# Stage two's way-back products in two halves of 64 stationary columns

## The chip, the cores and the metric

The kernel runs on one core of a Trainium2 chip. The metric is the device time of one execution in microseconds (us); what is compared is the median of several runs. The core's engines run side by side, each with its own order of instructions: PE (TensorE: matmuls, and beside them PEld, the load of the stationary operand), DVE (VectorE), ACT (ScalarE), POOL (GpSimd), and SP, which issues DMA transfers, as ACT and POOL do too. Operands lie in SBUF, an on-chip memory of 128 partitions; matmuls write to PSUM, whose banks hold 512 float32 values in each of 128 partitions.

A matmul `matmul(out, a, b)` computes the transpose of `a` times `b`. `a` is the stationary operand: its columns are loaded into the array and become the partitions of `out`. `b` is the moving operand: its columns stream through. In the profile `128*64 128x512` is a matmul with 128 partitions and 64 stationary columns, through which 512 moving columns stream.

## The reference

A block with two parts on `x` of 2048 rows and 512 columns: a spectral filter between two normalisations, then a dense layer with Mish and another dense layer. The change touches the first part alone.

```python
def _A_ref(x, w_r, w_i):
    X = rfft2(x, axes=(-2, -1))
    X = X * (w_r + 1j * w_i)
    return irfft2(X, s=(S, D), axes=(-2, -1))
...
h = _layernorm(x, axis=-1) * (1 + ca) + sa
x = x + ga * _A_ref(h, A_w_r, A_w_i)
h = _layernorm(x, axis=-1) * (1 + cb) + sb
x = x + gb * _B_ref(h, B_w1, B_b1, B_w2)
```

All inputs and outputs are float32.

## The kernel before

The two-dimensional Fourier transform is split into matmuls with small tables. Stage one (to about 50 us) takes the rows apart and does a transform of length 128 over the partitions; its result for each of 64 frequencies q of the row transform lies in the tile `a_sb`, 128 values in each of 128 partitions.

Stage two (about 50 to 90 us) works on groups of these frequencies, listed in `groups`: group 0 holds q = 0, group 1 the three of q = 1 to 3, and fifteen further groups hold four each. `seq` is the order in which they are taken: 1, 2, 3, 4, 0, 5, and so on. For each group, in this order:

- `p2_in` (L521) transposes the group's frequencies by four matmuls with `ident` (L528) into a bank "A", and ACT copies them out (L531). POOL adds a small correction to one column (L539).
- `p2_mul` (L541) multiplies by the table `kf`: one matmul with 512 moving columns (L548) into a bank "B" or "C".
- `p2_prod` (L562) multiplies by the spectral weights, a complex product: ACT copies the halves with their parts exchanged (L579, L580), POOL and DVE multiply (L581, L582).
- `p2_add` (L585): DVE adds the two products into the group's own place in `a_sb` (L588).
- `p2_out` (L590): the way back. For each of the group's `nq` frequencies a matmul (L597) with the 128 columns of that frequency in `a_sb` as the stationary operand and the first 128 columns of the table `kv` as the moving one. They write the columns `i * P` to `(i + 1) * P` of one bank "D", of which there are two. P is 128.
- `store_d` (L432) empties that bank into the tiles `dd[0]` and `dd[1]`, with a negated copy of a part: ACT by L441 and L443, in some groups DVE by L439 and L445 and POOL by L447.

Group 0 has its own way through `z_in`, `z_mul`, `z_prod`, `z_back` and `z_out`. `z_mul` and `z_out` call `reflected` (L463), which adds up several products in one bank: L464 and L468 with 128 stationary columns, L465 with a single column that writes one partition, and in `z_out` L467, whose operands have 96 partitions.

The order of the work is written out by hand: the loop over `s` at L648 is a software pipeline, and each engine works through its instructions in the order in which this loop issues them. In step `s` PE gets the table product of group `seq[s + 1]`, then the transposes of group `seq[s + 4]`, then the way-back products of group `seq[s - 3]`. From s = 13 on no transposes are left, and from s = 16 on no table products: the way-back products of the last five groups (s = 15 to 19) follow one another. DMA transfers of spectral weights (L630) are issued from ACT's queue within the same loop, as are those of the table `kc` (L686).

Stage three (from about 90 us) first does the column products of the inverse transform (L830 and L831, which read `dd` and `kc`), the row products (L840), and then both dense layers, whose matmuls (L942, L1045 and others) fill the time up to the end. Its order is a list of steps, `ORDER`, sorted by hand; the change doesn't touch it.

The change stands in `p2_out`. In the profile a product of float32 operands is two records, each with a weight load; so the 63 products of L597 are 126 matmuls and 126 weight loads.

Of the kernel before, what the change touches and what calls it, by code (L numbers as in the profile page):

```python
# [12 lines left out]
P = 128  # L13
# [69 lines left out]
def tile_spectral_block(ctx: ExitStack, tc: tile.TileContext, x_d, w1_d, b1_d, w2_d,  # L83
                        c_d, xt_d, wm_d, wq_d, wz_d, kr_d, km_d, kc_d, ki_d, kf_d, kv_d, kw_d, kp_d, out_d):
    nc = tc.nc
# [26 lines left out]
    def bank(tag):  # L112
        return psum.tile([P, 512], F32, name="bank", tag=tag)
# [38 lines left out]
    kv = pw.tile([P, 512], F32, name="kv")  # L152
# [279 lines left out]
    def store_d(ps, q0, nq, kind="all"):  # L432
        src = ps[:, 0:nq * 128].rearrange("p (q a c) -> p a c q", q=nq, c=2)
        for i in range(2):
            dst = dd[i].rearrange("p n d c q -> p (n d) c q")
            s = src[:, 32 * i:32 * i + 32]
            to, minus = dst[:, :, 0:2, q0:q0 + nq], dst[:, :, 2, q0:q0 + nq]
            if kind == "free" and i:
                nc.vector.tensor_copy(to, s)  # L439
            else:  # L440
                nc.scalar.copy(to, s)  # L441
            if kind == "all":
                nc.scalar.mul(minus, s[:, :, 0, :], -1.0)  # L443
            elif kind != "pool" and i:
                nc.vector.tensor_scalar(minus, s[:, :, 0, :], -1.0, None, op0=ALU.mult)  # L445
            else:
                nc.gpsimd.tensor_scalar(minus, dst[:, :, 0, q0:q0 + nq], -1.0, None, op0=ALU.mult)  # L447
# [67 lines left out]
    def z_out():  # L515
        t1, t2 = st.pop(("t", 0))
        pe = bank("D")
        reflected(pe[:, 0:P], t1, lambda i: kv[:, 128 + i * P:256 + i * P], [(t2[0:96, 0:P], kw)])
        store_d(pe, 0, 1)
# [33 lines left out]
    def slot(g):  # L553
        q0, nq = groups[g]
        return a_sb[:, q0:q0 + nq].rearrange("p q n e -> p (q n e)")
# [34 lines left out]
    def p2_out(g, kind):  # L590
        if g == 0:
            return z_out()
        q0, nq = groups[g]
        y = slot(g)
        pd = bank("D")
        for i in range(nq):
            nc.tensor.matmul(pd[:, i * P:(i + 1) * P], y[:, i * P:(i + 1) * P], kv[:, 0:128],  # L597
                             start=True, stop=True)
        store_d(pd, q0, nq, "all" if nq < 4 else kind)

    late = {}
# [30 lines left out]
    with tc.manual_schedule():  # L632
# [15 lines left out]
        for s in range(1, len(seq) + 3):  # L648
# [26 lines left out]
            if s >= 3:  # L675
                p2_out(seq[s - 3], "all" if s > 15 else "pool" if s > 13 else "busy" if work_mod[s] else "free")
# [566 lines left out]
    start = {}  # L1243
# [239 lines left out]
```

## Time and profile before

| | |
|---|---|
| time, median of three runs | 372.47 us (372.26 to 372.69) |
| the profiled execution | 372.4 us |
| its span, first to last instruction | 370.5 us |
| mean granted TensorE clock | 0.997 of full speed |
| PE busy | 363.6 us, 98% of the span |
| DVE, ACT, POOL busy | 309.9, 253.6, 64.8 us |
| way-back products, L597 | 126 matmuls of 272 to 377 ns, between 58.6 and 89.7 us |

Rows of the profile read as follows. A row of a timeline gives the start in us from the first instruction, the length in us, the engine, the line of the kernel, the operation, its output and inputs by name, their shapes, and how many instructions are merged in the row; in brackets stands how long the engine was idle before it and what ended that idle time. A row of grouped instructions gives after the bar the busy time in us and the mean length of one in ns, and then the idle time before them. A row of a stretch gives its bounds in us, its length, and for each engine the busy time and the number of instructions, and at the end the granted clock, the busy share of the DMA engines and the rate in GB/s. "issue" as a releaser is time in which the engine waited for nothing that the profile shows. Matmuls are pipelined and their ends are modelled, so the difference between starts says more than the length.

### The profile page before, as it was taken

What the parts mean: (1) busy time and instruction counts of PE and PEld (TensorE: products, weight loads), DVE (VectorE), ACT (ScalarE), POOL (GpSimd) and SP (SyncE); (2) the same over time, 40 slices, a digit from 0 to 9 for tenths busy, and PEclk for the clock granted to TensorE, in tenths of its full rate; (3) what the DMA queues carried; (4) which work ended last, traced back from release to release, by engine and by line L of the source; (5) the groups of instructions that cost most, each with busy time, mean ns of one, the idle gap of its engine ahead of it and who ended that gap; (6) DMA issues with size and microseconds to landing.
All of it is one profiled execution on the core that took longest, in us unless ns stands there. A gap on an engine that the chain in (4) does not pass through costs nothing.

```text
span 370.5 us, 8169 instructions
## 1 busy us (share of the span) xinstructions
PE 363.6 (98%) x2884; PEld 348.6 (94%) x2884; DVE 309.9 (84%) x760; ACT 253.6 (68%) x553; POOL 64.8 (17%) x102
## 2 busy tenths in 40 slices
PE   8999999998999999999999999999999999999995
PEld 8989977777999999999999999999999999999994
DVE  1898967888898899999898868996768978867896
ACT  1698879996557789789575778765686744555750
POOL 0478738786000000000001000000000000000000
PEclk9999999999999999999999999999999999999998
DMA  7999998777624656856978699775996797936032
GB/s 233 380 340 350 346 389 264 239 177 288 230 85 143 227 193 226 284 178 222 316 237 219 199 282 271 238 211 168 291 303 224 196 306 227 296 121 176 15 58 113
DMA packets 50888, 85.79 MB, mean 232 GB/s; under 512 B 7169, under 2 KB 18529, under 8 KB 50593
## 3 DMA queue, kind: packets, MB, share of 16 engines
q1 hardware_dynamic: 47680, 74.65, 60.2%
q10 hardware_dynamic: 2160, 6.95, 6.0%
q0 software_dynamic: 1008, 3.67, 5.9%
q8 instruction: 23, 0.38, 0.4%
q14 instruction: 17, 0.13, 0.1%
HBM read 66.12 MB, written 15.47 MB: 220 GB/s over the span
## 4 chain that ended last, share of the span: by engine, by line
PE 84%; DVE 7%; ACT 5%; issue 2%; ACTq 1%; POOL 0%; DVEq 0%
PE bank L942 28%; PE bank L1045 24%; PE bank L830 4%; PE bank L840 4%; PE bank L831 4%; PE bank L258 4%; PE bank L991 3%; PE bank L303 3%; PE bank L1041 3%; ACT buf L580 1%; PE bank L314 1%; PE bank L305 1%; PE bank L304 1%; ACT buf L579 1%; ACT d L441 1%
## 5 line engine op out<-in xcount | busy, mean ns | idle before, releaser
L1097 POOL DMA_DIRECT2D x<-modr x7 | 6.2, 888 | 260.2 <-DVE st L172 104.5
L942 PE MATMUL bank<-hT,wr 128*128 128x256 f32 x360 | 51.7, 283 | 0.0
L942 PEld LDWEIGHTS bank<-hT,wr 128*128 128x128 f32 x360 | 46.9, 192 | 0.1
L942 PE MATMUL bank<-hB,wr 128*128 128x256 f32 x300 | 43.4, 284 | 0.0
L942 PEld LDWEIGHTS bank<-hB,wr 128*128 128x128 f32 x300 | 39.1, 191 | 0.0
L1045 PE MATMUL bank<-w2a,ah 128*128 128x256 f32 x161 | 35.3, 283 | 0.0
L878 DVE TENSOR_TENSOR al<-buf,ah 128x512 fp32r<-128x512 f32 (+1 forms) x45 | 29.7, 666 | 4.6 <-ACT ah L877 4.5
L1045 PE MATMUL bank<-w2b,ah 128*128 128x256 f32 x147 | 32.3, 283 | 0.0
L877 ACT CAST ah<-buf 128x512 fp32r<-128x512 f32 (+1 forms) x45 | 26.9, 602 | 5.6 <-PE bank L1045 3.2
L942 PE MATMUL bank<-hcr,wr 128*128 128x256 f32 x210 | 30.0, 283 | 0.0
L942 PEld LDWEIGHTS bank<-hcr,wr 128*128 128x128 f32 x210 | 27.2, 192 | 0.0
L1045 PEld LDWEIGHTS bank<-w2a,ah 128*128 128x128 f32 x161 | 26.8, 192 | 0.0
L830 PE MATMUL bank<-kc,d 128*128 128x128 f32 x128 | 24.9, 276 | 0.5 <-ACT d L441 0.5
L831 PE MATMUL bank<-kc,d 128*128 128x128 f32 x128 | 24.7, 275 | 0.0
L1045 PEld LDWEIGHTS bank<-w2b,ah 128*128 128x128 f32 x147 | 24.6, 191 | 0.0
L1045 PE MATMUL bank<-w,ah 128*128 128x256 f32 x112 | 22.0, 286 | 0.0
L172 DVE BATCH_NORM_STATS2 st<-x 128x6 f32<-128x512 f32 x32 | 21.9, 685 | 0.0
L303 PE MATMUL bank<-buf,mring 128*128 128x512 f32 x48 | 20.6, 430 | 0.2 <-DVE buf L296 0.2
L830 PEld LDWEIGHTS bank<-kc,d 128*128 128x128 f32 x128 | 19.4, 192 | 0.7 <-ACT d L441 0.7
L831 PEld LDWEIGHTS bank<-kc,d 128*128 128x128 f32 x128 | 19.4, 192 | 0.0
L597 PEld LDWEIGHTS bank<-kv,a_sb 128*128 128x128 f32 x126 | 15.4, 191 | 2.7 <-issue 2.2
L833 ACT COPY buf<-bank 128x512 f32<-128x512 f32 x16 | 9.3, 583 | 12.5 <-PE bank L831 12.5
(295 smaller groups left out, 1099.1 us busy)
## 6 DMA issues: line engine op xcount, KB each, us to landing
wr<-w_S SPq DMA_DIRECT2D x60, 256.0 KB, 3.7
wr<-w_A SPq DMA_DIRECT2D x45, 256.0 KB, 4.1
w_S<-hT SPq DMA_DIRECT2D x20, 256.0 KB, 2.0
x<-in_A_x_dram SPq DMA_DIRECT2D x16, 256.0 KB, 5.1
xring<-in_x_t_dram SPq DMA_DIRECT2D x16, 256.0 KB, 5.0
w_A<-wr SPq DMA_DIRECT2D x15, 256.0 KB, 2.6
x<-modr POOLq DMA_DIRECT2D x7, 512.0 KB, 5.6
out_dram<-x SPq DMA_DIRECT2D x7, 512.0 KB, 3.8
```

The lines of the kernel that those rows point to most:

```text
L172: nc.vector.bn_stats(t, x[:, n, :])
L258: nc.tensor.matmul(pgv[:, j], data(j), krs[:, j, :].rearrange("p (c q) -> p c q", c=2), start=True, stop=True)
L303: nc.tensor.matmul(pa, m[:, a, 0:128], g, start=(i == 0), stop=False)
L597: nc.tensor.matmul(pd[:, i * P:(i + 1) * P], y[:, i * P:(i + 1) * P], kv[:, 0:128], start=True, stop=True)
L830: nc.tensor.matmul(o, dj[:, 0:128], kc[0][:, n, :], start=True, stop=False)
L831: nc.tensor.matmul(o, dj[:, 64:192], kc[1][:, n, :], start=False, stop=True)
L840: nc.tensor.matmul(px[:, j * P:(j + 1) * P], e[:, j * P:(j + 1) * P], kiv[:, j, :], start=True, stop=True)
L877: nc.scalar.copy(h, r)
L878: nc.vector.tensor_tensor(l, r, plain(h), op=ALU.subtract)
L942: nc.tensor.matmul(o, w[:, p, k, :], h[:, q, k, :], start=(first and n == 0), stop=(last and n == 5), skip_group_check=True)
L991: nc.tensor.matmul(o, w1s[:, p, k, :], slots[f"B{k // 2 + 1}{s + 1}"][:, q, k % 2, :], start=(u == 0 and m == 0), stop=(m == 11), skip_gro ...
L1045: nc.tensor.matmul(out_ps[b][n][:, 256 * half:256 * half + 256], a[p][:, e], w2[t][q][:, r], start=(t == 1 and half == 0 and i == 0), stop ...
```

## The change

Each way-back product is issued as two: the first with the stationary columns 0 to 63 of the frequency, which writes partitions 0 to 63 of the output, the second with columns 64 to 127, which writes partitions 64 to 127. The moving operand is the same 128 columns of `kv` for both, and the columns of the bank are the same. The products are the same numbers as before. There are 126 products in place of 63; nothing else is different.

```diff
         for i in range(nq):
-            nc.tensor.matmul(pd[:, i * P:(i + 1) * P], y[:, i * P:(i + 1) * P], kv[:, 0:128],
-                             start=True, stop=True)
+            for lo in (0, P // 2):
+                nc.tensor.matmul(pd[lo:lo + P // 2, i * P:(i + 1) * P], y[:, i * P + lo:i * P + lo + P // 2], kv[:, 0:128],
+                                 start=True, stop=True)
         store_d(pd, q0, nq, "all" if nq < 4 else kind)
```

## The prediction

> **What bounds the kernel now.** I first read the page's head for the engine that is full, then the busy time by stretch for where it is full, then the matmul timeline for how it is filled.
>
> ```profile
> span 370.5 us, 8169 instructions
> PE 363.6 (98%) x2884; PEld 348.6 (94%) x2884; DVE 309.9 (84%) x760; ACT 253.6 (68%) x553; POOL 64.8 (17%) x102
> ```
>
> ```profile
> core 0: us, PE busy (x) PEld busy (x) DVE busy (x) ACT busy (x) POOL busy (x), PEclk, DMA share, GB/s
> 58.40:83.83 25.43, 25.43 (x159) 18.83 (x158) 21.66 (x51) 24.39 (x57) 20.66 (x36) 1.00 0.74 225
> 72.00:74.19 2.19, 2.19 (x17) 1.66 (x15) 1.59 (x3) 2.13 (x5) 1.74 (x4) 1.00 0.91 286
> 83.83:90.40 6.57, 5.24 (x42) 4.69 (x41) 6.36 (x12) 4.78 (x19) 4.33 (x7) 1.00 0.86 339
> 90.40:366.00 275.60, 275.60 (x2304) 274.38 (x2305) 236.85 (x583) 182.62 (x388) 6.99 (x8) 1.00 0.68 209
> ```
>
> PE is busy for 98% of the span. In the part of stage two that holds the first eleven groups of way-back products (58.40 to 83.83) it has no gap, and in everything after stage two (90.40 to 366.00) it has none either. Only the end of stage two, 83.83 to 90.40, leaves PE 1.33 us idle. The granted clock is 1.00 in all four, so no stretch here runs at a lower one. A busy PE may still be waiting inside its pipeline, so the starts decide:
>
> ```profile
> start us, us, engine line op out<-in xcount [idle before <-releaser]
> ...
> 57.47 0.44 PE L464 MATMUL bank<-kf,early 128*128 128x160 f32 x2
> 57.84 0.43 PE L465 MATMUL bank<-kf,early 128*1 128x160 f32 x2
> 58.20 0.54 PE L468 MATMUL bank<-kf,early 128*128 128x160 f32 x2
> 58.58 0.83 PE L597 MATMUL bank<-kv,a_sb 128*128 128x128 f32 x6
> 59.25 1.02 PE L548 MATMUL bank<-early,kf 128*128 128x512 f32 x2
> ...
> 62.74 0.27 PE L506 MATMUL bank<-ident,buf 128*128 128x128 f32 x1
> 62.84 0.27 PE L507 MATMUL bank<-ident,buf 128*96 128x128 f32 x1
> 62.95 1.06 PE L597 MATMUL bank<-kv,a_sb 128*128 128x128 f32 x8
> ...
> 67.34 0.39 PE L464 MATMUL bank<-kv,early 128*128 128x128 f32 x2
> 67.65 0.38 PE L465 MATMUL bank<-kv,early 128*1 128x128 f32 x2
> 67.96 0.49 PE L467 MATMUL bank<-kw,early 96*128 96x128 f32 x2
> 68.29 0.39 PE L468 MATMUL bank<-kv,early 128*128 128x128 f32 x2
> 68.51 1.02 PE L548 MATMUL bank<-buf,kf 128*128 128x512 f32 x2
> ...
> 74.19 1.06 PE L597 MATMUL bank<-kv,a_sb 128*128 128x128 f32 x8
> 75.08 1.02 PE L548 MATMUL bank<-buf,kf 128*128 128x512 f32 x2
> 75.94 0.60 PE L528 MATMUL bank<-ident,a_sb 128*128 128x128 f32 x4
> 76.38 1.06 PE L597 MATMUL bank<-kv,a_sb 128*128 128x128 f32 x8
> ...
> 82.08 1.05 PE L597 MATMUL bank<-kv,a_sb 128*128 128x128 f32 x8
> 82.97 1.02 PE L548 MATMUL bank<-buf,kf 128*128 128x512 f32 x2
> 83.83 4.26 PE L597 MATMUL bank<-kv,a_sb 128*128 128x128 f32 x32
> 88.81 1.13 PE L597 MATMUL bank<-kv,a_sb 128*128 128x128 f32 x8 [0.72 <-DVE a_sb L588]
> 90.40 0.49 PE L830 MATMUL bank<-kc,d 128*128 128x128 f32 x2 [0.46 <-ACT d L441]
> ```
>
> Starts matter here, not lengths: a matmul's length (1.06 for eight) holds its way through the array, which the next one overlaps. A float32 product stands in the trace as two records. One steady step goes from 74.19 to 76.38: eight L597 records to 75.08 (0.89 us), two L548 records to 75.94 (0.86), four transposes to 76.38 (0.44). The sum is the step, 2.19 us, so PE sets it. ACT is busy for 2.13 of such a step, only 0.06 behind. That is why the page's chain of waits passes much of this stage through ACT. A step made shorter would gain 0.06 at most, while a PE made slower is followed at once.
>
> **What a record costs.** Eight L597 records in 0.89 us are 0.111 us each, whole products 0.222. The change makes four records out of two: the same 128 moving columns twice, with 64 stationary columns each time.
>
> ```profile
> L597 PEld LDWEIGHTS bank<-kv,a_sb 128*128 128x128 f32 x126 | 15.4, 191 | 2.7 <-issue 2.2 <-ACT d L443 0.3 <-DVE d L445 0.2
> L991 PEld LDWEIGHTS bank<-hB,w1s 128*96 128x96 f32 x48 | 6.0, 163 | 0.0
> L465 PEld LDWEIGHTS bank<-kv,early 128*1 128x1 f32 x2 | 0.1, 80 | 0.1
> L465 PE MATMUL bank<-kv,early 128*1 128x128 f32 x2 | 0.4, 270 | 0.0
> ```
>
> A weight load becomes cheaper: 80 ns for 1 column, 163 for 96, 191 for 128 give 0.87 ns a column, so some 135 ns for 64, an estimate from these rows. A matmul record doesn't: with one stationary column L465 still lasts 270 ns against L597's 275 or so, and its pair lasts 0.38, so the second starts 0.11 after the first. The streaming of 128 moving columns sets the pace, and a narrower stationary side saves none of it.
>
> No row shows two half-width records on opposite halves, so the price of a split product has two ends. If the second half runs entirely beside the first, it is 0.222 as before, two records of 0.111 in each half, side by side. If one follows the other, it is 4 x 0.111 = 0.444. Less than 0.222 I exclude, since each half still streams two records of 0.111. I take 0.444: the nearest row is L465's, a narrow record that takes its full turn, and no row of this trace shows two matmuls abreast.
>
> **What entering and leaving costs.** L465 is also the one place where the used part of the array shrinks to a few columns and grows again. In the group from 67.34 to 68.51 four products of two records would need 8 x 0.111 = 0.89; they take 1.17, so 0.28 more. In the group from 57.47 to 58.58 three products with 160 moving columns would need 6 x 0.139 = 0.83; they take 1.11, again 0.28 more. At the entry the first record starts at 67.65, not at 67.56 (0.09 late); the other 0.19 is at the way out, where the wide weights aren't loaded ahead. With 96 columns no such delay shows: L507 starts 0.10 after L506, and L597 0.11 after L507. I put the same price on each group of split products. Its first weights add the difference of 64 columns over one (135 - 80 = 0.055 us), since they are loaded behind the drained array: 0.335 us in all, of which 0.145 at the entry. Its lower bound is nothing, if the stall belongs to L465's sharing its output addresses with L464; the upper bound is this price at every change of half (a rival below).
>
> **The sum.** The first eleven groups (one of three products from 58.58, ten of four, the last from 82.08) each have another kind of PE work before and behind them.
> - Ten groups of four: 8 more records, 0.89, and 0.335: 1.225 each, 12.25.
> - The group of three: 0.67 (58.58 to 59.25) becomes 1.33; with 0.335, 1.0.
> - The end: five groups follow one another from 83.83, with one entry for all. Before, 83.83 to L830's start at 90.40 took 6.57, with PE waiting for DVE before the last group. After: 0.145 + 5 x 1.78 + 0.70 (from the last record's turn, 88.81 + 0.89 = 89.70, to 90.40) = 9.75, so +3.18. The exit's 0.19 lies inside the 0.70, in which PE waits for ACT.
>
> ```profile
> 87.97 0.69 DVE L588 TENSOR_TENSOR a_sb<-bank,buf 128x512 f32<-128x512 f32 x1
> ```
>
> ```profile
> 88.56 0.38 ACT L441 COPY d<-bank 128x256 f32<-128x256 f32 x1
> 88.81 0.31 ACT L443 ACTIVATE d<-bank 128x128 f32<-128x128 f32 x1
> ```
>
> DVE's last sum is ready at 88.66, 4.83 after the last L548 has had its turn; the slower PE asks for it after 0.145 + 4 x 1.78 = 7.27. That wait is gone, and PE sets the end as well. ACT empties half a group's bank in some 0.56 us (88.56 to the end of L443 at 89.12), both halves in 1.1, less than the 1.78 that PE takes for a group, so bank D's two buffers hold nothing up.
>
> Together 12.25 + 1.0 + 3.18 = 16.4 us. What else the change moves costs nothing: no DMA, no copy, no wait is added, and the copies of store_d, the weight fetches on ACT's queue and POOL's sums have 1.2 us more per step than now. Since PE has no gap from 90.40 to 366.00, what stage two loses cannot be made up, and the shift reaches the end whole. The profiled execution took 372.4 us, 1.9 around its span of 370.5, and the median of the runs is 372.47. So the forecast is 388.9 us (372.47 + 16.4).
>
> **The rivals.**
> - *The halves run abreast.* Split product 0.222, plus one record (0.111) at a group's end that has no partner, plus 0.335: 0.445 for each of eleven groups, 4.9; at the end only the last record, 0.1, since the wait for DVE stays. +5.0, 377.5. For it: the two halves share no output partition and no stationary column. Against: no row shows it. The Trainium skill has this as a rule (TensorEngine Tiling (Array Packing), Key Properties): different tiles of the array load weights and multiply in parallel. By that rule the time would be this rival's; no run here shows it so far.
> - *Half abreast.* The second half's weights (0.055) are loaded only once the record before has begun, and likewise back: 0.055 + 0.111 per half, 0.332 a product. Groups of four 0.44 + 0.335, of three 0.33 + 0.335: 8.4; the end 0.145 + 5 x 1.33 + 0.70 - 6.57 = 0.9. +9.3, 381.8.
> - *Each change of half drains the array* (0.145, as at L465's entry). Seven changes in a group of four, five in one of three, 39 at the end: +10.15, +0.73 and +5.66 on top of 16.4: 33 us, 405. Against: L465 is a change of width, and the halves are equal. The skill speaks against it too: the same section has the drain at a change of the tiling mode, not of the tile. The 0.28 us at L465 agree with its first half; nothing here shows the second.
> - *The split doesn't reach the array*: half records run as full-width ones, without entry or exit, as the 96-column loads do. 9.57 + (5 x 1.78 + 0.70 - 6.57) = 12.6, 385.1.
> - *Not slower.* The halves run abreast and the drain belongs to L465's shared addresses alone; the unpartnered record is then overlapped by the next L548. Each group costs nothing, 372.5. It decides as long as entry, exit and the last record stay below 0.067 us a group (0.2% of the time, 0.74 us, over eleven); ACT's 2.13 in a step of 2.19 caps a gain near 0.06 a step, some 0.5 us. Against: the same 0.28 in both groups with L465, while L467 and L468 share addresses too and L468 starts without delay.
>
> **Chances.** The forecast 0.43, abreast 0.28, half abreast 0.13, drain at each change 0.05, no split in the array 0.04, not slower 0.07. The range reaches from below the abreast case (377.5) to above the forecast: 376.5 to 391. It leaves out the drain case and the last one, 0.12. About 0.2% is what a measurement of this kernel tells from no change: faster 0.02 and same 0.05 from the last case, slower 0.93.
>
> **What would show it.** L597 should have 252 records of each kind, weight loads near 135 ns, matmuls still near 275. The step from one L597 group to the next should be 3.4 us (2.19 now); 2.6 speaks for abreast, 3.0 for half abreast, 4.4 for a drain at each change. Within a group, the starts should be 0.111 apart with no overlap between halves; pairs that start together would refute me. A gap of about 0.15 before the group's first record and 0.19 behind its last would bear out the entry and exit. L830 should start near 106.8, without the 0.72 wait for DVE, and the stretch behind it should last as long as now. A group that takes 0.9 to 1.0 us would make the prediction wrong at its largest term.

## The result and the profile after

The changed kernel took 375.03 us in the median of four runs (374.69 to 375.55), the kernel before 372.51 (372.26 to 372.69): a ratio of 1.0069 with a 95% interval of 1.0053 to 1.0085. It is slower by 2.5 us. The prediction had the sign, but 16.4 us and a range from 376.5 that leaves 375.03 out.

The head of the page of the changed kernel, and its two groups of way-back products (L598 is the old L597; lines behind it are one higher too), with the matmuls of the kernel before as the last row:

```profile
span 372.9 us, 8421 instructions
PE 366.6 (98%) x3010; PEld 346.8 (93%) x3010; DVE 310.2 (83%) x760; ACT 253.8 (68%) x553; POOL 65.0 (17%) x102
```

```profile
L598 PE MATMUL bank<-kv,a_sb 128*64 128x128 f32 x252 | 16.8, 279 | 0.1
L598 PEld LDWEIGHTS bank<-kv,a_sb 128*64 128x64 f32 x252 | 13.4, 136 | 4.4 <-ACT d L441 1.5 <-issue 1.0 <-DVE bank L582 0.8
...
L597 PE MATMUL bank<-kv,a_sb 128*128 128x128 f32 x126 | 16.6, 277 | 0.9 <-DVE a_sb L588 0.7
```

There are twice as many records, each weight load lasts 136 ns (estimated: 135), each matmul about as long as before (279 ns, 277). Yet together they keep PE busy for 16.8 us, against 16.6 before. The matmul timeline of the changed kernel, a steady step and the end of stage two (start, length, engine, line):

```profile
73.58 1.13 PE L548 MATMUL bank<-buf,kf 128*128 128x512 f32 x2
74.54 0.60 PE L528 MATMUL bank<-ident,a_sb 128*128 128x128 f32 x4
75.07 1.09 PE L598 MATMUL bank<-kv,a_sb 128*64 128x128 f32 x16
76.10 1.12 PE L548 MATMUL bank<-buf,kf 128*128 128x512 f32 x2
...
81.13 1.13 PE L548 MATMUL bank<-buf,kf 128*128 128x512 f32 x2
...
83.21 1.13 PE L548 MATMUL bank<-buf,kf 128*128 128x512 f32 x2
84.27 1.09 PE L598 MATMUL bank<-kv,a_sb 128*64 128x128 f32 x16
85.29 1.13 PE L548 MATMUL bank<-buf,kf 128*128 128x512 f32 x2
86.35 5.13 PE L598 MATMUL bank<-kv,a_sb 128*64 128x128 f32 x80
91.95 0.49 PE L831 MATMUL bank<-kc,d 128*128 128x128 f32 x2 [0.47 <-ACT d L441]
```

Sixteen records take 1.09 us from the first start to the last end, where eight took 1.06. The step, from 73.58 to 76.10, is 2.52 us (2.19 before). The first records of one group, in a stretch cut just behind the first start and in a longer one:

```profile
75.07 0.32 PE L598 MATMUL bank<-kv,a_sb 128*64 128x128 f32 x1
...
75.07 0.33 PE L598 MATMUL bank<-kv,a_sb 128*64 128x128 f32 x2
```

One record reaches to 75.39, two to 75.40: both start within 0.01 us. The rows don't name the half of a record, but two records of one half never start that close (they are 0.109 us apart, see run 1 below), so these two belong to different halves. The halves run abreast, from the first record on; eight pairs follow one another at 0.109 us.

What is left of the 2.52 us is the change of width. The fourth transpose's turn ends at 74.54 + 0.44 = 74.98, and the first pair starts 0.09 later. From it to the next L548 are 1.03, where eight pairs need 0.87: 0.05 for the first narrow load, which nothing covers, and 0.10 before the wide product starts. That product then lasts 1.12 to 1.13 in place of 1.02, as its own first load is uncovered. Together 0.09 + 0.16 + 0.11 = 0.36, less 0.02 for the slightly quicker pairs: the 0.33 us by which the step grew.

Stage two in both profiles, cut at the first L464, the start of the last L548 record, and the first column product of stage three (the first two rows are of the kernel before, the others of the changed one; columns as in the prediction's stretches):

```profile
57.47:83.40 25.93, 25.93 (x164) 19.20 (x162) 22.19 (x51) 24.85 (x59) 20.80 (x37) 1.00 0.75 227
83.40:90.40 7.00, 5.67 (x43) 4.80 (x41) 6.66 (x14) 5.21 (x19) 4.76 (x8) 1.00 0.85 337
```

```profile
56.30:85.83 29.53, 29.53 (x250) 18.83 (x248) 23.45 (x53) 25.67 (x60) 21.83 (x39) 1.00 0.69 212
85.83:91.95 6.12, 5.52 (x83) 4.29 (x81) 5.17 (x11) 4.42 (x18) 3.49 (x6) 1.00 0.83 317
```

The head grew by 3.6 us, eleven times 0.33; the end shrank by 0.9, where PE's idle time fell from 1.33 to 0.60. The sum, 2.7, is the 2.5 us of the runs. The two spans differ by 2.4, since besides stage two began 1.17 us earlier and stage three lasted 0.85 longer (280.95 against 280.11); experiment 4 and the other profiles show both to vary.

What PE waits for at the end is no longer DVE. DVE's last sum is ready 4.21 us after the start of the last L548 record, where it was 5.26, and so in time for the last group. The wait that is left among the way-back products is for a bank D that ACT has still to empty; the kernel before had one like it (0.34 us):

```profile
89.41 1.82 PEld L598 LDWEIGHTS bank<-kv,a_sb 128*64 128x64 f32 x32 [0.37 <-ACT d L443]
```

So the prediction's "bank D's two buffers hold nothing up" held only for the slow groups that it expected.

### The profile page after: what moved, and what is told of

Read it like the earlier page. It is cut to its first block, busy times and chain, and to the rows that moved or that the text cites. A ratio compares the mean times of both kernels' runs of the same rounds, so it can differ in the third digit from the quotient of the medians.

```text
span 372.9 us, 8421 instructions
## 1 busy us (share of the span) xinstructions
PE 366.6 (98%) x3010; PEld 346.8 (93%) x3010; DVE 310.2 (83%) x760; ACT 253.8 (68%) x553; POOL 65.0 (17%) x102
## 4 chain that ended last, share of the span: by engine, by line
PE 88%; DVE 7%; DMA 2%; issue 1%; ACT 1%; DVEq 0%; ACTq 0%
PE bank L943 26%; PE bank L1046 22%; PE bank L548 4%; PE bank L831 4%; PE bank L841 4%; PE bank L832 4%; PE bank L598 4%; PE bank L258 4%; PE bank L992 3%; PE bank L303 3%; PE bank L1042 2%; PE bank L528 2%; DMA w_S<-hT 2%; PE bank L305 1%; PE bank L304 1%
## 5 line engine op out<-in xcount | busy, mean ns | idle before, releaser
L879 DVE TENSOR_TENSOR al<-buf,ah 128x512 fp32r<-128x512 f32 (+1 forms) x45 | 29.7, 665 | 4.6 <-ACT ah L878 4.5
L598 PEld LDWEIGHTS bank<-kv,a_sb 128*64 128x64 f32 x252 | 13.4, 136 | 4.4 <-ACT d L441 1.5
```

The lines of the kernel that those rows point to most:

```text
L598: nc.tensor.matmul(pd[lo:lo + P // 2, i * P:(i + 1) * P], y[:, i * P + lo:i * P + lo + P // 2], kv[:, 0:128], start=True, stop=True)
L879: nc.vector.tensor_tensor(l, r, plain(h), op=ALU.subtract)
```

## The experiments

All of them in one table, from their profiles; "head", "end" and "stage three" are cut as above, "step" is from one L548 to the next in the steady part. Ratios are to the kernel before on the same chip, with their intervals; without one, the time is of a single run. Each run's stages are read from one profile.

| run | step | head | end | stage two | stage three | time, ratio |
|---|---|---|---|---|---|---|
| before | 2.19 | 25.93 | 7.00 | 32.9 | 280.1 | 372.51 |
| the change | 2.52 | 29.53 | 6.12 | 35.7 | 281.0 | 375.03, 1.0069 (1.0053 to 1.0085) |
| 1 low halves first | 3.01 | 34.7 | 7.6 | 42.2 | 280.8 | 381.93, 1.0252 (1.0216 to 1.0288) |
| 2 one product of a group | 2.53 | 29.7 | 7.0 | 36.7 | 280.7 | 376.53, 1.0094 (1.0066 to 1.0121) |
| 3 wide column | 2.19 | 25.8 | 7.4 | 33.2 | 281.3 | 373.19, 1.0008 (0.9994 to 1.0023) |
| 4 before again | 2.19 | 25.9 | 7.1 | 33.0 | 281.2 | 373.45 |
| 5 first eleven groups | 2.52 | 29.5 | 6.1 | 35.6 | 281.4 | 377.21, 1.0098 (1.0066 to 1.0130) |
| 6 last five groups | 2.19 | 25.9 | 7.0 | 32.9 | 280.6 | 372.33, 0.9983 (0.9962 to 1.0004) |
| 7 every other product | 2.87 | 33.4 | 8.9 | 42.4 | 281.1 | 382.67 |
| 8 two by two | 2.57 | 30.0 | 6.2 | 36.3 | 280.9 | 376.02 |
| 9 narrow table product | 2.47 | 28.5 | 7.1 | 35.6 | 280.7 | 375.35 |
| 10 quarters | 2.50 | 29.4 | 6.4 | 35.7 | 281.2 | 375.27 |
| 11 wide column, copies moved | 2.19 | 25.8 | 7.5 | 33.4 | 280.6 | 373.56, 1.0023 (1.0008 to 1.0037) |
| 12 one copy moved | 2.19 | 25.9 | 7.0 | 32.9 | 281.2 | 372.97, 0.9996 (0.9983 to 1.0009) |

**1. How the halves come abreast.**

```diff
-        for i in range(nq):
-            for lo in (0, P // 2):
+        for lo in (0, P // 2):
+            for i in range(nq):
```

> The same products as the change, but all low halves of a group first, then all its high halves. Theory 1 (TensorE picks records for the two halves only among near neighbours in the order): eight records of one half follow one another at 0.109 us, then eight of the other, so a group takes about 1.75 us and the step 2.52 + 0.87 = 3.4 us; eleven steps and the end make about +13 us on 375.0, near 388. Theory 2 (a record of 64 columns lasts half as long whatever its neighbours): the records follow at 0.055, the step stays at 2.52 and the time near 375. Theory 3 (each half has a queue of its own that looks past eight records of the other): pairs as now, step 2.52, near 375, but with low and high records starting together.

None of the three. The step came to 3.01 us. The steady group of this run, whole, and in two stretches from its start, of 0.43 and 0.50 us:

```profile
72.67 1.58 PE L598 MATMUL bank<-kv,a_sb 128*64 128x128 f32 x16
74.19 1.13 PE L548 MATMUL bank<-buf,kf 128*128 128x512 f32 x2
...
72.67 0.65 PE L598 MATMUL bank<-kv,a_sb 128*64 128x128 f32 x4
...
72.67 0.82 PE L598 MATMUL bank<-kv,a_sb 128*64 128x128 f32 x6
```

Four records start alone, the second 0.16 us behind the first and the others 0.109 apart. Then the fifth low record and the first high one, which is ninth in the order, start within 0.01 us of each other (the fifth and sixth record of the last row). From there on low and high run abreast, and the last four high ones are alone: twelve turns in place of eight, 4 x 0.109 = 0.44 of the 0.49 by which the step grew over 2.52. The other 0.05 fits a first load of the high half that nothing covers: the second high record, too, starts 0.16 behind the first. So records of one half do follow one another at the full 0.109, and a high record may start ahead of low ones that stand before it in the order, but here no more than four records ahead: the ninth beside the fifth.

**8. The reach tested.** Low, low, high, high for two frequencies at a time:

```diff
-        for i in range(nq):
-            for lo in (0, P // 2):
+        for i, lo in [(i, lo) for k in range(0, nq, 2) for lo in (0, P // 2) for i in range(k, min(k + 2, nq))]:
+            if True:
```

> All products are split, in the order low, low, high, high for two frequencies at a time, so that four records of one half stand together (two with the change, eight with all low halves first). With all low first, the first high record started beside the fifth low one, as if PE looked past four records. If that is the reach, four records together are still within it: the first high record starts beside the first low one, or one record later at most, and the step stays at 2.52 to 2.63 us. If the reach depends on the halves of a whole group, the first high record starts beside the third low one, and the step is 2.74.

The step was 2.57 and the first high record, fifth in the order, started 0.014 us behind the first low one. Like the ninth beside the fifth in run 1, the fifth beside the first agrees with a reach of four records. Run 10 below shows that it isn't a plain distance in the order.

**2 and 7. Is it the narrow records or the change of width?** Only the last product of a group split, and every other one (both against the kernel before):

```diff
-            nc.tensor.matmul(pd[:, i * P:(i + 1) * P], y[:, i * P:(i + 1) * P], kv[:, 0:128],
-                             start=True, stop=True)
+            wide = P if i < nq - 1 else P // 2
+            for lo in range(0, P, wide):
+                nc.tensor.matmul(pd[lo:lo + wide, i * P:(i + 1) * P], y[:, i * P + lo:i * P + lo + wide], kv[:, 0:128],
+                                 start=True, stop=True)
```

> Only the last product of each group is split, the others keep 128 stationary columns. Theory A (the cost is the entry to and the exit from the narrow form, once per group): the group still pays 0.33 us, the step stays near 2.52 us and the time near 375. At the end, where five groups follow one another, each has its own entry and exit now (five instead of one), so up to 1 us more there. Theory B (each narrow record costs a little): a quarter of the cost, a step of 2.27 us and a time near 373.1.

> In each group every other product is split (0 and 2), the products 1 and 3 keep 128 stationary columns: half as many narrow records as in the change, but two entries and two exits per group. Theory A: twice 0.33 us per group, a step of 2.19 + 0.66 = 2.85 us (2.52 with the change), and about 3.6 us more than the change, near 378.5. Theory B: half of the change's cost, a step of 2.35.

(Experiment 7 has `i % 2` for the condition.) A quarter of the narrow records cost as much per step as all of them, 2.53 us; half of them, in two stretches, cost twice as much over 2.19: 2.87. That is theory A to 0.02 us. At the end run 2 paid its 0.9 for five entries in place of one. Run 7 missed its total, 382.67 against 378.5: I had counted the eleven groups of the head alone, and at the end two entries and exits in each of five groups took another 2.8 us over the change's 6.12. Of the 4.2 us missed, another 0.3 lies in the head, and 1.1 outside stage two, where single executions vary.

**3. Is the delay at L465 the same thing?** L465 multiplies by 128 columns, of which 127 are zero, and not by one. This is against the kernel before; the lines by which POOL prepares `column` are left out:

```diff
-        nc.tensor.matmul(out[0:1], t[:, 0:1], w(2), start=False, stop=False)
+        nc.tensor.matmul(out, column, w(2), start=False, stop=False)
```

> The kernel before, with L465's single stationary column replaced by 128 columns of which 127 are zeros; three small POOL operations and one more memset prepare them. The output addresses are still shared with L464 and L468. Theory A (the delay at L465 comes from the change of width): both groups lose their 0.28 us, 0.83 and 0.89 remain, and the time falls by 0.5 us or less, to about 372.0. Theory C (the delay comes from adding onto the addresses that L464 has just written): nothing changes, 1.11 and 1.17 us remain and the time stays at 372.5.

The later of the two groups in this run:

```profile
67.02 0.39 PE L464 MATMUL bank<-kv,early 128*128 128x128 f32 x2
67.24 0.39 PE L465 MATMUL bank<-kv,early 128*128 128x128 f32 x2
67.47 0.39 PE L467 MATMUL bank<-kw,early 96*128 96x128 f32 x2
67.69 0.39 PE L468 MATMUL bank<-kv,early 128*128 128x128 f32 x2
67.91 1.02 PE L551 MATMUL bank<-buf,kf 128*128 128x512 f32 x2
```

The starts are 0.22 apart, and 1.17 us became 0.89, with the output addresses as shared as before. The delay was the width's. In the earlier group, from 57.15, 1.11 became 0.92 and not the 0.83 expected: its second record starts 0.24 us behind the first, the others 0.136 apart, so one wide load is uncovered there. The rest of the expectation failed: the time didn't fall. Of the nearly 0.5 us that PE saved, most turned up as gaps later in the stage, 0.09 before a table product at 80.71 and 0.29 before the group at 83.68, and stage two took 33.2.

**4. What varies by itself.**

> The kernel before, unchanged, for a second profile. In the two profiles at hand the first L464 starts at 57.47 us before the change and at 56.30 after it, and stage three lasts 280.1 and 280.95 us. If these 1.17 and 0.85 us vary from execution to execution, this profile differs from the first by several tenths in either part; if they belong to the change, it repeats 57.5 and 280.1 within 0.2.

The first L464 came at 57.47 again, but stage three took 281.2 us, 1.1 more than in the first profile of the same kernel. Over all fourteen profiles it lay between 280.1 and 281.4, and the first L464 between 56.3 and 58.3 us, with no relation to the edits behind it. I take differences of this size outside stage two as chance; stage two itself came to 32.92 and 32.99.

**5 and 6. Which groups cost.** The condition of run 2 with `seq.index(g) >= 12`, then `< 12`:

> Only the first eleven groups are split, the last five keep 128 stationary columns. Theory A with an end set by DVE: eleven entries and exits of 0.33 us cost 3.6, and some 1.0 of it falls into the wait for DVE before the last group, as in the change: about +2.6 us, near the change's own time (ratio 1.006 to 1.008). Theory B (the narrow records of all sixteen groups cost): eleven sixteenths of the change's 2.5 us, 1.7 (ratio 1.0046).

> Only the last five groups are split, which follow one another at the end of stage two. Theory A with an end set by DVE: one entry for all five, inside time in which PE waits for DVE anyway, so the wait of 0.72 before the last group gets shorter and the time stays at that of the kernel before (ratio 1.000, within 0.002). Theory B: five sixteenths of 2.5, +0.8 us (ratio 1.002).

Stage two took 35.6 us with the first eleven split, as much as the change, and 32.9 with the last five split, as much as the kernel before. The ratios of run 5 and of the change agree within their intervals, and theory B's 1.0046 lies below that of run 5; that of run 6 includes 1.000, so it isn't shown to be faster. The last five cost nothing, the first eleven everything.

**9 and 10. Narrow neighbours, narrower pieces.** Run 9 splits the table product too, on top of the change:

```diff
-        nc.tensor.matmul(pb[:, 0:w], kf[:, 0:128], z[:, 0:w], start=True, stop=True)
+        for lo in (0, P // 2):
+            nc.tensor.matmul(pb[lo:lo + P // 2, 0:w], kf[:, lo:lo + P // 2], z[:, 0:w], start=True, stop=True)
```

(Experiment 10 is the change with `range(0, P, P // 4)` and pieces of `P // 4` columns.)

> The change, and the table product L548 split in two halves of 64 stationary columns as well, so that the way-back products and the table product behind them have the same width. Theory A (the price is the change of width, and narrow records cost nothing): a steady step still has one entry and one exit, now between the table product and the transposes, and stays near 2.52 us; the steps without transposes (three before the last table product) have none and fall from 2.08 to about 1.75 us. From the first L464 to the last L548 28.5 us instead of 29.5. Theory B (each narrow record costs): the four records of a narrow table product make each step longer than 2.52.

> Each product as four of 32 stationary columns. If the quarters run four abreast, a group still takes eight records' time, 0.87 us, and the step is 2.5 to 2.7 us, as the reach of some four records may delay the fourth quarter a little. If only two run abreast, sixteen records' time, 1.75 us, and a step of 3.4.

With the table product as narrow as its neighbours, the steps without transposes fell as expected:

```profile
81.89 1.03 PE L549 MATMUL bank<-buf,kf 128*64 128x512 f32 x4
82.75 1.04 PE L599 MATMUL bank<-kv,a_sb 128*64 128x128 f32 x16
83.63 1.03 PE L549 MATMUL bank<-buf,kf 128*64 128x512 f32 x4
84.48 1.04 PE L599 MATMUL bank<-kv,a_sb 128*64 128x128 f32 x16
85.36 1.03 PE L549 MATMUL bank<-buf,kf 128*64 128x512 f32 x4
```

81.89 to 83.63 is 1.74 us, as in the kernel before. So narrow records cost nothing where no width changes. But the head's 1.0 us came back at the end (7.1 for 6.12), with a wait of 0.84 for DVE before the last group. In the quarters a group of 32 records stands in 1.08 us:

```profile
72.71 1.08 PE L598 MATMUL bank<-kv,a_sb 128*32 128x128 f32 x32
73.72 1.12 PE L548 MATMUL bank<-buf,kf 128*128 128x512 f32 x2
...
72.71 0.32 PE L598 MATMUL bank<-kv,a_sb 128*32 128x128 f32 x4
```

Four ran abreast, and the step was 2.50. The last row is of a stretch cut 0.03 us behind the first start: four records have started in it, one of each quarter. A product's two records stand together in the order, so the fourth quarter's first record is the seventh, and yet it starts beside the first. A reach of four records in the order can't be, then. What fits runs 1, 8 and 10 is that each half or quarter takes up to some four records, one running and three waiting, and that the order is held up only by a record whose half is full: in run 1 the eighth low record finds room when the fifth starts, and the ninth follows at once. No run tried this by itself.

**11 and 12. What waits at the end of stage two.** Run 11 adds to run 3 that the copies of step 13 go from DVE to ACT and POOL (`"pool" if s > 12`); run 12 moves one of them, to ACT (`"busy" if work_mod[s] or s == 13`):

> The kernel before with the wide column (which took the two delays of 0.28 us from PE and left the time where it was, since the last group's products waited for DVE as before) and with the copies of the group in step 13 moved from DVE to ACT and POOL: DVE has 0.70 us less ahead of the chain that ends stage two. If DVE's backlog sets the end of stage two, 0.5 to 0.7 us are gained there: stage two 32.3 to 32.5 us instead of 32.9, the time about 0.15% below the kernel before. If ACT or POOL, which get the copies, set it, nothing is gained.

> The kernel before, with the copy of one half of the bank in step 13 (L439, 0.41 us) moved from DVE to ACT; DVE keeps the negated copy and POOL gets nothing, unlike the run that moved both and made POOL late. If DVE's backlog sets the end of stage two, the last sum is ready 0.3 to 0.4 us earlier and stage two takes about 32.6 us instead of 32.9 or 33.0; the whole time falls by 0.1%, less than these runs can tell. If POOL's product is what DVE waits for, nothing is gained.

In both the branch in which nothing is gained came out, and neither run beats the kernel before. In run 12 DVE, with less to do, waits for POOL:

```profile
82.76 0.29 DVE L445 TENSOR_SCALAR d<-bank 128x128 f32<-128x128 f32 x1
83.45 0.69 DVE L588 TENSOR_TENSOR a_sb<-bank,buf 128x512 f32<-128x512 f32 x1 [0.40 <-POOL buf L581]
```

The last sum is ready 4.84 us after the last L548's turn, as in the kernel before. It isn't DVE's load alone that sets the end, but ACT, POOL and DVE in turn. POOL's product L581 shows their pace, in the kernel before and in the changed one:

```profile
77.98 1.27 POOL L581 TENSOR_TENSOR buf<-buf,wqa 128x512 f32<-128x512 f32 x1 [0.45 <-ACT buf L580]
...
80.07 1.28 POOL L581 TENSOR_TENSOR buf<-buf,wqb 128x512 f32<-128x512 f32 x1 [0.17 <-ACT buf L580]
...
82.43 1.27 POOL L581 TENSOR_TENSOR buf<-buf,wqb 128x512 f32<-128x512 f32 x1 [0.45 <-ACT buf L580]
...
84.17 1.27 POOL L581 TENSOR_TENSOR buf<-buf,wqb 128x512 f32<-128x512 f32 x1
```

```profile
83.56 1.28 POOL L581 TENSOR_TENSOR buf<-buf,wqb 128x512 f32<-128x512 f32 x1 [0.60 <-ACT buf L580]
...
85.64 1.27 POOL L581 TENSOR_TENSOR buf<-buf,wqb 128x512 f32<-128x512 f32 x1 [0.31 <-ACT buf L580]
```

Before, (84.17 - 77.98) / 3 = 2.06 us per step, while PE's table products in the last two steps came every 1.75 (79.46, 81.22, 82.97): PE ran ahead without a gap and then waited at the end. With the change PE comes every 2.08 there (81.13, 83.21, 85.29) and POOL too. About 2 x 0.33 of PE's loss fell into time that it would have waited. Which of the three sets the 2.06 isn't shown. ACT is the fullest, busy for 9.37 of the 9.64 us from 74.19 to 83.83 in the kernel before (DVE 8.53, POOL 8.39), but runs 11 and 12 gave it more work, and no run gave it less.

## Why the prediction was wrong

- *What bounds the kernel now.* Right for the steady steps: each of them grew by PE's 0.33 us. Wrong in "In the part of stage two that holds the first eleven groups of way-back products (58.40 to 83.83) it has no gap", taken as a bound for all eleven. In the last two steps before 83.83 PE had no gap because it ran ahead; the bill was the 0.72 us wait at 88.81, which I had quoted, and which I let the slow forecast swallow rather than carry into each case. The rival of halves abreast kept 0.1 us for the end; it was -0.9.
- *What a record costs.* The step that failed is "I take 0.444: the nearest row is L465's". L465 shows what a narrow record takes after one of its own half, and that is right: 0.109 in run 1. It can't show what a record of the other half does, since both of its records use the same column. Taken to mean that all four follow one another, it put 0.444 where the runs show 0.218, and with it 12.6 of the 16.4 us (the working of the rival without a split has them). That the sign came out right rests on the other 3.8, the entry and exit. The weight load of 64 columns was 136 ns for an estimated 135.
- *What entering and leaving costs.* Right: 0.335 forecast, 0.33 in the step, 0.34 per visit in run 7. The reserve that it might belong to L465's addresses fell with run 3.
- *The rivals.* "The halves run abreast" was the right one, with 377.5. It was 2.5 us too slow, 2.2 of it for two reasons: the unpartnered record of 0.111 in each of eleven groups, 1.2 us, doesn't exist, since PE starts the second half at once; and the covered end, 1.0 us. The rule on which it rested, that different tiles of the array load weights and multiply in parallel (the Trainium skill, TensorEngine Tiling (Array Packing), Key Properties), agrees with the pairs 0.01 us apart and with run 10's 32 records in 1.08 us. The drain at a change of mode, not of the tile, which the prediction cites from the same section of the Trainium skill, agrees with 0.09 to 0.10 us at each change of width and pairs 0.109 us apart without a gap between halves. "Half abreast", "each change of half drains" and "the split doesn't reach the array" are refuted by the pairs' 0.109 and by the 136 ns loads. "Not slower" failed at the 0.33 us per group.
- *After stage two.* "The shift reaches the end whole" held: stage two lost 2.7 us, the runs 2.5.
- *The range* was built to reach just below the abreast case with that case's own errors left out: its two terms that were bounds from above, the lone record and the end, deserved their lower ends.

## What to carry to other kernels

Splitting a product of 128 stationary columns into narrower ones gains nothing by itself: the pieces run side by side, and each still streams all the moving columns. What costs is every change between narrow and wide products, here 0.33 us for a visit, so narrow products belong together, and a single one among wide ones costs as much as a whole group. An engine without gaps bounds a step only if what it feeds keeps its pace; if a wait stands at the end of the stage, the steps before it have slack, and a saving there turns up as a wait, as it did in runs 3 and 9.

## What the runs showed of the hardware

The order in which matmuls are issued isn't kept between halves of the array. In run 1 the ninth record started beside the fifth, in run 8 the fifth beside the first. The Trainium skill says otherwise (TensorE: Matmul & The Clock Gate, The mechanism: matmuls start and end in program order); these traces disagree where records go to different column halves or quarters. How far a record may run ahead is open: four places in the order in runs 1 and 8, six in run 10, which fits some four records held for each piece. And float32 products of 64 and of 32 columns run two and four abreast, with pairs 0.109 us apart against 0.111 for full-width records.
